# Moving the second batch's later pieces by eight visits, reordering ACT's ramp steps, and halving two products with their turns

## The chip, the cores and the metric

The kernel runs on one NeuronCore of a Trainium2 chip. Its engines work side by side, each through its own instruction list in order: PE (TensorE) multiplies matrices into the eight PSUM banks, ACT (ScalarE) and DVE (VectorE) read PSUM and SBUF, POOL (GpSimd) reads SBUF only, and SP (SyncE) issues the DMAs. An instruction that waits holds up everything behind it on its engine or queue. The metric is the device time of one execution in microseconds (us).

## The reference

For each of 4 batches of 12480 rows x of 128 numbers, two attentions and then a two-layer network:

```
h   = mab(I, x)          # 32 inducing rows attend to the batch
y   = mab(x, h)          # the batch attends to these 32 rows
# mab(q, kv): s = q kv^T / sqrt(128); a = softmax(s); a @ kv
g   = prelu(y @ w_in)    # 128 -> 2048, a slope alpha for each of the 2048
out = g @ w_out          # 2048 -> 128
```

Since y is a @ h with a of 32 columns, the kernel computes HW = h @ w_in once per batch, and then a @ HW in place of y @ w_in. The network's nonlinear part is relu(a @ HW) @ W1 with W1 = (1 - alpha) w_out; its linear part is a @ HA with HA = h @ (w_in alpha w_out).

## The kernel before

**Tiling.** A batch is cut into six rows of the schedule, called supers s = 0 to 5, of 16 tiles of 128 rows each, and a remainder of 192 rows. A super (b, s) of the second attention is four blocks of four tiles. The network of one block takes four visits; a visit makes 4 of the 16 chunks of the hidden layer. There are 390 visits in one chain: super (0, 0) has visits 0 to 15, (0, 1) has 16 to 31, (0, 2) has 32 to 47, (0, 3) begins at 48, and the second batch begins at visit 96.

**A visit** (`visit`, line 808): four matmuls `hh<-a,HW` that run side by side on 32 rows of the array each; four relus from PSUM into `gt` tiles, on ACT (line 821) or DVE (line 823); then `second` (line 834), the 16 matmuls of the visit before into the block's sums; and then the steps that hang on this visit. Every eighth visit, two blocks' linear parts (line 861) come between. A block's finished sums are copied into `ob` and stored by SP (lines 880 to 897).

**Steps.** `at(n, fn, ...)` hangs a step on visit n; steps of the same visit run in the order in which they were hung. A planner (`Plan`) goes through all visits with the steps' listed costs and chooses for each relu and copy whether ACT or DVE does it, and for each other step of these two engines whether it stays where it hangs or waits until after the second relu of the next visit (`plan.then`). It doesn't know POOL, the DMAs, or which step needs the result of which. What is hung on POOL and SP runs in the order of the list.

**A super of the second attention** takes these steps at the eight visits of `when`: `b_scores` (PE, line 644, and a copy out, lines 702 and 704), `b_max` (DVE, line 721), `b_less_pool` (POOL, line 726), `b_exp` (ACT, line 688), `b_sum` (POOL, lines 712 and 736), `b_rec` (DVE, line 749: one reciprocal for each softmax row), `b_mul` (POOL, line 757: exponentials times reciprocals, repeated four times into `rep`), and `b_turn` (SP, line 766: a transposing DMA of `rep` into the tile `a2`, "a" in the profile, which the visits' matmuls read). The one `rep` buffer of this kind serves all supers. For (0, 1) `when` is written out by hand, since there is no room for the usual lead of 23 visits. The first super (0, 0) is made in the ramp ahead of visit 0 and divides by its softmax sums only in the block's copy (line 880, with the reciprocals of `first_rec`, line 1173).

**The first attention of the next batch** is made between the visits in seven pieces p: p = 0 is super 0, p = 1 the remainder, p = 2 to 6 supers 1 to 5. Each piece has `a_load` (SP, line 315 or 320), a cast to bf16 (POOL, line 330; for p = 0 of the second batch four parts on ACT, line 347), `a_turn` (SP, line 356, a transposing DMA into `xT`), `a_scores_least` (PE line 379, DVE lines 393 and 402), `a_exp` (ACT, line 418), `a_e1` (SP, line 449, a transposing DMA), `a_fac` (ACT, line 436) and the join `a_h_add` (PE line 473, DVE lines 487 and 489). Behind the last join stand `a_max`, `a_factors`, `a_parts`, `a_den` (lines 508 to 573), `a_sum` (PE line 582, DVE line 587: the new h, `hT`), and `a_w_both` and `a_lin` (lines 598 to 621: HW and HA). The first `b_scores` of the second batch hangs on visit 73 and reads `hT`.

All loads, stores and transposing DMAs but the last store go through SP's one list, in the order in which the steps are hung.

Of the kernel before, what the change touches and what calls it, by code (L numbers as in the profile page):

```python
# [21 lines left out]
P = 128  # L22
R = 4
ST = 16
# [6 lines left out]
def kernel(  # L31
# [11 lines left out]
    bf16 = mybir.dt.bfloat16  # L43

    B, N, C = x.shape
    M = inducing.shape[0]
# [10 lines left out]
    if left:  # L57
        nt = -(-left // P)
        supers.append((len(supers) * ST * P, nt, left - (nt - 1) * P))
    NS = len(supers)  # L60
# [26 lines left out]
    H = ST // 2  # L87
# [14 lines left out]
    rep_pool = ctx.enter_context(tc.tile_pool(name="rep", bufs=1))  # L102
# [183 lines left out]
    def new_state(b):  # L286
        st = State()
        st.b = b
        st.pieces = whole_pieces if b else first_pieces
        st.np = len(st.pieces)  # L290
        st.xT = xt_pool.tile([C, NT, P], bf16, name="xT", tag="xT")
        st.xn, st.xs, st.s1, st.e1T, st.e1, st.s1p, st.hp = {}, {}, {}, {}, {}, {}, {}
        st.e2, st.m2, st.den2, st.rc, st.rep = {}, {}, {}, {}, {}

        st.mx = sm_pool.tile([P, NX], f32, name="mx", tag="mx")
        st.rm = sm_pool.tile([P, NX], f32, name="rm", tag="rm")
        st.fac = sm_pool.tile([P, NX], f32, name="fac", tag="fac")
        st.da = sm_pool.tile([P, NX], f32, name="da", tag="da")
        st.ex = sm_pool.tile([P, NX], f32, name="ex", tag="ex")
        st.den = sm_pool.tile([P, 1], f32, name="den", tag="den")  # L300
        st.hs = h_pool.tile([P, C], f32, name="hs", tag="hs")
        eng = nc.gpsimd if b else nc.vector
        eng.memset(st.mx[:], HIGH)
        eng.memset(st.da[:], 0.0)
        return st
# [320 lines left out]
    def a2_of(b, s):  # L626
        if (b, s) not in a2s:
            a2s[b, s] = a2_pool.tile([P, ST, P], bf16, name="a2", tag="a2")
        return a2s[b, s]
# [56 lines left out]
    def b_exp(e, n):  # L686
        def work():
            nc.scalar.activation(out=e[:, :n], in_=e[:, :n], func=EXP, scale=scale)  # L688

        plan.then(work)  # L690
# [60 lines left out]
        plan.then(work)  # L751
        st.rc[s] = rc

    def b_mul(st, s, n):
        rc = st.rc[s]
        rep = rep_pool.tile([P, ST, R, M], bf16, name="rep", tag="rep")
        nc.gpsimd.tensor_tensor(  # L757
            out=rep[:, :n],
            in0=st.e2[s][:, :n].unsqueeze(2).broadcast_to([P, n, R, M]),
            in1=rc[:, :n].unsqueeze(2).unsqueeze(3).broadcast_to([P, n, R, M]),  # L760
            op=MULT,
        )
        st.rep[s] = rep

    def b_turn(st, s, t0, n):
        nc.sync.dma_start_transpose(
            out=a2_of(st.b, s)[:, t0 : t0 + n, :],
            in_=st.rep[s][:, :n].rearrange("p t r m -> p (t r m)"),
        )

    def b_exp_once(e, n, w):
# [138 lines left out]
    st = new_state(0)  # L910
    xs_left = const.tile([P, supers[-1][1], C], f32, name="xs_left")
    for pc in first_pieces[:5]:
# [20 lines left out]
        out=mask[:], in_=ident32[:].rearrange("k (g m) -> k m g", g=R), axis=AX, op=ADD  # L933
# [3 lines left out]
        out=group[:], in_=ident32[:].rearrange("k (g m) -> k g m", g=R), axis=AX, op=ADD  # L937
# [5 lines left out]
        out=low[:], in0=mask[:], scalar1=-1.0, scalar2=HIGH, op0=ADD, op1=MULT  # L943
# [3 lines left out]
        out=nident[:], in0=ident32[:], scalar1=-1.0, scalar2=None, op0=MULT  # L947
# [255 lines left out]
    def at(n, fn, *args, cost=()):  # L1203


        todo.setdefault(max(n, 0), []).append((fn, args, cost))
# [1 line left out]
    at(2, rest_exp, H, H, cost=[("a", 560), ("!", 0)])  # L1208
    at(0, first_turn, cost=[("s", 350), ("f", 0)])
    at(2, first_turn_dma)  # L1210
    at(6, first_rec, cost=[("v", 160)])
    at(5, linear_product, cost=[("s", 900), ("v", 210), ("!", 0)])
    at(6, a_lin, st, cost=[("s", 260), ("v", 210)])
    blocks[0].later = True
# [4 lines left out]
    for b, s, nt in groups[1:]:  # L1219
        n = first[b, s]  # L1220
        when = [n - 23, n - 19, n - 16, n - 14, n - 13, n - 11, n - 9, n - 6]
        if (b, s) == (0, 1):
            when = [0, 2, 3, 4, 5, 8, 8, 8]
        if (b, s) == (0, 2):
            when[7] = n - 7
        at(when[0], on, b, b_scores, s, nt, cost=[("s", 25 * nt), ("f", 0)])
        at(when[1], on, b, b_max, s, nt, cost=[("v", 70 + 33 * nt)])
        at(when[2], on, b, b_less_pool, s, nt)
        at(
            when[3],  # L1230
            lambda b=b, s=s, nt=nt: b_exp(states[b].e2[s], nt),
            cost=[("a", 100 + 27 * nt)],
        )
        at(when[4], on, b, b_sum, s, nt)
        at(when[5], on, b, b_rec, s, nt, cost=[("v", 160)])
        at(when[6], on, b, b_mul, s, nt)
        at(when[7], on, b, b_turn, s, 0, nt)
    at(3, first_sum)
    for part in range(3):
        at(first[B, 0] - 50 + 8 * part, tails, part)  # L1240
# [3 lines left out]
    def small_at(n, fn, *args, cost):  # L1244


        (kind, ns), *rest = cost
        at(n, fn, *args, cost=[(kind, ns + (0 if n in shared else TURNED)), *rest])
        shared.add(n)

    for b in range(B - 1):
        n = first[b, 0] - 1
        if b:
            at(n - 4, lambda b=b: states.__setitem__(b + 1, new_state(b + 1)))
        for p, pc in enumerate(whole_pieces):
            m = n + (8 * (p - 1) if p > 1 else p)
            load, cast, turn = m - 3, m + 6, m + 8
            score = m + 15 if p > 1 else n + 16
            look = score + 1 + (p == 1)
            join = m + (24 if p == whole_pieces[-1].k else 23) if p > 1 else n + (31 if p else 23)  # L1260
            if not b:
                load, cast, turn = {
                    0: (-1, -1, 7), 1: (-1, 9, 10), 2: (4, 9, 11), 3: (12, 20, 21)
                }.get(p, (load, cast, turn))
                score, look = (score, look) if p > 1 else (score + 4, look + 4)
                join = n + 31 if p < 2 else n + 39 if p < 4 else join
            f = pc.full
            if load >= 0:
                at(load, on, b + 1, a_load, pc)
            if cast >= 0:  # L1270
                at(cast, on, b + 1, a_cast, pc)
            else:
                for q, v in enumerate((4, 5, 5, 6)):
                    at(v, on, b + 1, a_cast_act, pc, q * BT, BT, cost=[("a", 560)])
            at(turn, on, b + 1, a_turn, pc)
            small_at(
                score,
                on,
                b + 1,
                a_scores_least,  # L1280
                pc,
                cost=[("s", 215 if f else 85), ("v", 800 if f else 460)],
            )
            at(look, on, b + 1, a_exp, pc, cost=[("a", 717 if f else 430)])
            at(look + 2, on, b + 1, a_fac, pc, cost=[("a", 220)] if p else [])
            at(look + 1, on, b + 1, a_e1, pc)
            small_at(
                join, on, b + 1, a_h_add, pc, cost=[("s", 226 if f else 115), ("v", 260)]
            )
        m = n + 8 * (NS - 2) + 15  # L1290
        at(m + 2, on, b + 1, a_max, cost=[("a", 200)])
        at(m + 4, on, b + 1, a_factors, cost=[("s", 400), ("v", 70), ("a", 205)])
        at(m + 6, on, b + 1, a_parts, cost=[("a", 220), ("v", 260)])
        at(m + 8, on, b + 1, a_den, cost=[("s", 200), ("v", 370)])
        at(m + 12, on, b + 1, a_sum, cost=[("s", 200), ("v", 110)])
        small_at(m + 14, on, b + 1, a_w_both, cost=[("s", 220), ("a", 487)])
        small_at(m + 14, on, b + 1, a_lin, cost=[("s", 75), ("v", 190)])

# [3 lines left out]
    for n, (blk, i) in enumerate(visits):  # L1302
        before = visits[n - 1][0] if n else None
        nt = before.nt * before.per if n else 0
# [7 lines left out]
        cost = nt * Plan.FREE if both else 0  # L1312
# [55 lines left out]
```

## Time and profile before

| what | value |
|---|---|
| median of 3 runs | 596.29 us (595.6 to 596.78) |
| profiled execution | 597.49 us |
| its span | 595.6 us |
| PE busy | 585.8 us (98%) |
| DVE busy | 535.9 us (90%) |
| ACT busy | 537.4 us (90%) |
| POOL busy | 216.7 us (36%) |
| mean granted clock of TensorE | 0.997 |

The profile shows one execution. A row of the timeline has the start, the duration, the engine, the line, the operation with the tile written and those read, and the number of instructions merged; in brackets stands the engine's idle time ahead of it and what ended that. In the rows of SP the duration is that of the issue; when the transfer has landed is told by another view, the DMA issues, as the time from issue to landing. The granted clock is the share of full speed that TensorE was given.

### The profile page before, as it was taken

Reading aid. Unit: us, or ns where it says so; the run is one execution under the profiler, and the core shown is the slowest. Engines: PE = TensorE matmul, PEld = TensorE weight load, DVE = VectorE, ACT = ScalarE, POOL = GpSimd, SP = SyncE. Lnnn points to the kernel's source line nnn. Section 1 sums busy time; section 2 is a strip of 40 time slices with the busy share of each in tenths; the row PEclk is TensorE's granted clock in tenths of the full one; section 3 lists DMA queues with packets and bytes.
Section 4 is the critical chain, followed back from the end, with each engine's and each line's share of the span. In section 5 each row is a group of like instructions: output and inputs, shape, how many; then the busy total and the mean of one; then the engine's idle time right before and its main releaser. Section 6 shows DMA issues by size and latency. Waiting matters only on the chain.

```text
span 595.6 us, 23148 instructions
## 1 busy us (share of the span) xinstructions
PE 585.8 (98%) x9500; PEld 442.1 (74%) x9500; DVE 535.9 (90%) x978; ACT 537.4 (90%) x1085; POOL 216.7 (36%) x260
## 2 busy tenths in 40 slices
PE   9999979999999999999999999999999999999997
PEld 6677757777777777777777777777777777777776
DVE  5899979998999899989999989999999999999996
ACT  5789969999999999999989999999999999999986
POOL 3484615403416336223236165133133134144010
PEclk9999989999999999999999999999999999999999
DMA  8957999332167999641367989731331331433421
GB/s 337 274 171 148 245 228 195 74 100 72 56 185 173 223 199 215 134 82 39 89 150 174 202 213 227 167 82 55 90 73 55 91 63 65 118 73 68 91 69 47
DMA packets 122347, 80.56 MB, mean 135 GB/s; under 512 B 103760, under 2 KB 106112, under 8 KB 119168
## 3 DMA queue, kind: packets, MB, share of 16 engines
q1 hardware_dynamic: 122016, 78.99, 55.8%
q8 instruction: 74, 1.21, 0.9%
q14 instruction: 33, 0.27, 0.2%
q10 hardware_dynamic: 224, 0.09, 0.1%
HBM read 28.07 MB, written 25.56 MB: 90 GB/s over the span
## 4 chain that ended last, share of the span: by engine, by line
PE 94%; DMA 4%; DVE 1%; ACT 0%; issue 0%; DVEq 0%; POOL 0%; SPq 0%
PE bp L834 64%; PE hh L808 21%; DMA xs<-in_x_dram 3%; PE bp L861 2%; PE hh L644 2%; PE hh L473 1%; DMA a<-rep 1%; PE hh L379 1%; DVE gt L823 1%; PE bp L963 1%; PE hh L364 0%; PE hh L598 0%; PE hh L456 0%; DVEq L1363 0%; DVE xn L349 0%
## 5 line engine op out<-in xcount | busy, mean ns | idle before, releaser
L821 ACT ACTIVATE gt<-hh 128x512 bf16<-128x512 f32 x853 | 454.5, 604 | 39.2 <-PE hh L808 34.2
L823 DVE TENSOR_SCALAR gt<-hh 128x512 bf16<-128x512 f32 x707 | 454.1, 683 | 28.7 <-PE hh L808 17.6
L834 PE MATMUL bp<-W,gt 128*128 128x128 bf16 x6240 | 418.1, 220 | 0.2 <-DVE gt L823 0.2
L834 PEld LDWEIGHTS <-gt 128*128 128x128 bf16 x6240 | 350.4, 98 | 84.7 <-issue 77.2
L808 PE MATMUL hh<-a,HW 32*128 32x512 bf16 (+2 forms) x1664 | 156.8, 371 | 3.2 <-DMA a<-rep 3.1
L757 POOL TENSOR_TENSOR rep<-e,rc 128x2048 bf16<-128x2048 f32 (+1 forms) x24 | 84.5, 3521 | 24.4 <-DVE rc L749 23.4
L726 POOL TENSOR_TENSOR e<-e,smx 128x512 f32<-128x512 f32 (+1 forms) x24 | 24.6, 1026 | 154.6 <-ACT gt L821 88.6
L808 PEld LDWEIGHTS <-HW 32*128 32x128 bf16 x1664 | 40.5, 91 | 45.2 <-issue 6.3
L712 POOL TENSOR_TENSOR t<-e 128x256 f32<-128x256 f32 (+1 forms) x24 | 17.2, 718 | 144.4 <-ACT e L688 144.3
L887 ACT COPY ob<-bp 128x512 f32<-128x512 f32 (+1 forms) x62 | 36.3, 585 | 4.5 <-PE bp L834 1.6
L330 POOL CAST xn<-xs 128x2048 bf16<-128x2048 f32 x17 | 32.1, 1890 | 3.5 <-DMA xs<-in_x_dram 3.1
L712 POOL TENSOR_TENSOR t<-t 128x128 f32<-128x128 f32 (+3 forms) x100 | 30.4, 304 | 7.8
L889 DVE COPY ob<-bp 128x512 f32<-128x512 f32 x32 | 21.9, 684 | 6.1 <-PE bp L834 6.1
L393 DVE TENSOR_SCALAR_CACHE_REDUCE s<-hh 128x512 f32<-128x512 f32 (+2 forms) x29 | 17.9, 619 | 1.6 <-PE hh L379 1.6
L861 PEld LDWEIGHTS <-a 32*128 32x128 bf16 x392 | 15.0, 93 | 5.8 <-issue 0.2
L861 PE MATMUL bp<-HA,a 32*128 32x128 bf16 x392 | 19.1, 214 | 0.0
L418 ACT ACTIVATE e1T<-s,rm 128x512 bf16<-128x512 f32 (+1 forms) x25 | 17.9, 715 | 0.4 <-DVE rm L402 0.2
L721 DVE TENSOR_REDUCE smx<-e 128x16 f32<-128x512 f32 (+1 forms) x24 | 15.9, 661 | 0.0
L688 ACT ACTIVATE e<-e 128x512 f32<-128x512 f32 (+1 forms) x24 | 15.0, 624 | 0.8 <-POOL e L726 0.8
L963 PE MATMUL bp<-blank 128*128 128x256 bf16 x78 | 13.8, 311 | 1.2 <-DVE blank L909 1.2
L489 DVE SCALAR_TENSOR_TENSOR hs<-hs,fac,hh 128x128 f32<-128x128 f32 (+1 forms) x25 | 8.6, 344 | 6.2 <-PE hh L473 5.5
L702 ACT COPY e<-hh 128x512 f32<-128x512 f32 (+1 forms) x22 | 13.4, 607 | 0.0
(109 smaller groups left out, 204.1 us busy)
## 6 DMA issues: line engine op xcount, KB each, us to landing
out_dram<-ob SPq DMA_DIRECT2D x97, 256.0 KB, 2.6
xs<-in_x_dram SPq DMA_DIRECT2D x23, 1024.0 KB, 6.4
xs<-in_x_dram SPq DMA_DIRECT2D x2, 512.0 KB, 9.2
w_in_f<-in_moe_w_in_dram SPq DMA_DIRECT2D x1, 1024.0 KB, 4.8
a<-rep SPq DMA_TRANSPOSE x25, 4.9
xT<-xn SPq DMA_TRANSPOSE x18, 6.1
e<-e1T SPq DMA_TRANSPOSE x18, 3.1
xs_left<-in_x_dram SPq DMA_DIRECT2D x4, 64.0 KB, 5.1
```

The costliest lines, as they stand in the source:

```text
L330: nc.gpsimd.tensor_copy(out=st.xn[s][:], in_=xs[:])
L712: nc.gpsimd.tensor_tensor(out=t[:, :n], in0=src[:, :n, :w], in1=src[:, :n, w : 2 * w], op=ADD)
L726: nc.gpsimd.tensor_tensor(out=st.e2[s][:, :n], in0=st.e2[s][:, :n], in1=st.m2[s][:, :n].unsqueeze(2).broadcast_to([P, n, M]), op=SUB,)
L757: nc.gpsimd.tensor_tensor(out=rep[:, :n], in0=st.e2[s][:, :n].unsqueeze(2).broadcast_to([P, n, R, M]), in1=rc[:, :n].unsqueeze(2).unsqueez ...
L808: nc.tensor.matmul(hh[:, q * cols + w.start : q * cols + w.stop], HWs[b][rows, v * P : (v + 1) * P], a2[rows, t0 : t0 + nt, :].rearrange(" ...
L821: nc.scalar.activation(out=gt[:, :cols], in_=hh[:, :cols], func=RELU)
L823: nc.vector.tensor_relu(gt[:, :cols], hh[:, :cols])
L834: nc.tensor.matmul(blk.acc[:, t * C : (t + 1) * C], gt[:, (q * nt + t) * P : (q * nt + t + 1) * P], W1[:, k, :], start=(not blk.begun), st ...
L861: nc.tensor.matmul(blk.acc[w, t * C : (t + 1) * C], blk.a2[rows, blk.t0 + t, w], HAs[b][rows, :], start=(not blk.begun and t == 0), stop=F ...
L887: nc.scalar.copy(out=ob[:, :nt], in_=acc)
L889: nc.vector.tensor_copy(out=ob[:, :nt], in_=acc)
L963: nc.tensor.matmul(ps[:, : 2 * P], blank[:, :P], blank[:], start=True, stop=True)
```

## The change

- `b_mul` and `b_turn` work on `n` tiles from `t0`, and for (0, 1) and (0, 2) each is called for tiles 0 to 7 and for tiles 8 to 15. For (0, 1), where both hang on visit 8, the order is product, turn, product, turn; for (0, 2) the two products hang on visit 23 and the two turns on visit 25.
- For (0, 1) `b_exp` goes from visit 4 to 6 and `b_sum` from 5 to 7; the reciprocal, product and turn stay at 8. The four ACT casts of the second batch's piece 0 go from visits 4, 5, 5, 6 to 3, 4, 5, 5, its turn from 7 to 6, and `first_rec` from 6 to 7.
- In the second batch the pieces 3 to 6 come eight visits later in all their steps (piece 3's load, cast and turn go from 12, 20, 21 to 20, 29, 31; its join from 38 to 46), and so do the steps behind the last join, `a_sum` alone by six: from 66 to 72. `a_w_both` and `a_lin` go from 68 to 76.

```diff
-    def b_mul(st, s, n):
-        rc = st.rc[s]
-        rep = rep_pool.tile([P, ST, R, M], bf16, name="rep", tag="rep")
+    def b_mul(st, s, n, t0=0):
+        rc, ts = st.rc[s], slice(t0, t0 + n)
+        if not t0:
+            st.rep[s] = rep_pool.tile([P, ST, R, M], bf16, name="rep", tag="rep")
         nc.gpsimd.tensor_tensor(
-            out=rep[:, :n],
+            out=st.rep[s][:, ts],
...
     def b_turn(st, s, t0, n):
         nc.sync.dma_start_transpose(
             out=a2_of(st.b, s)[:, t0 : t0 + n, :],
-            in_=st.rep[s][:, :n].rearrange("p t r m -> p (t r m)"),
+            in_=st.rep[s][:, t0 : t0 + n].rearrange("p t r m -> p (t r m)"),
...
-    at(6, first_rec, cost=[("v", 160)])
+    at(7, first_rec, cost=[("v", 160)])
...
         if (b, s) == (0, 1):
-            when = [0, 2, 3, 4, 5, 8, 8, 8]
+            when = [0, 2, 3, 6, 7, 8, 8, 8]
...
-        at(when[6], on, b, b_mul, s, nt)
-        at(when[7], on, b, b_turn, s, 0, nt)
+        parts = [(0, H), (H, H)] if (b, s) in ((0, 1), (0, 2)) else [(0, nt)]
+        for t0, n in parts:
+            at(when[6], on, b, b_mul, s, n, t0)
+            if when[6] == when[7]:
+                at(when[7], on, b, b_turn, s, t0, n)
+        if when[6] != when[7]:
+            for t0, n in parts:
+                at(when[7], on, b, b_turn, s, t0, n)
...
-            m = n + (8 * (p - 1) if p > 1 else p)
+            m = n + (8 * (p - 1 + (not b and p > 2)) if p > 1 else p)
...
-                    0: (-1, -1, 7), 1: (-1, 9, 10), 2: (4, 9, 11), 3: (12, 20, 21)
+                    0: (-1, -1, 6), 1: (-1, 9, 10), 2: (4, 9, 11)
...
-                join = n + 31 if p < 2 else n + 39 if p < 4 else join
+                join = n + 31 if p < 2 else n + 39 if p < 3 else join
...
-                for q, v in enumerate((4, 5, 5, 6)):
+                for q, v in enumerate((3, 4, 5, 5)):
...
-        m = n + 8 * (NS - 2) + 15
+        m = n + 8 * (NS - 2 + (not b)) + 15
...
-        at(m + 12, on, b + 1, a_sum, cost=[("s", 200), ("v", 110)])
+        at(m + (12 if b else 10), on, b + 1, a_sum, cost=[("s", 200), ("v", 110)])
```

More of the change, by code (lines that the diff above doesn't have):

```diff
@@ L752, in b_rec @@
         st.rc[s] = rc
-    def b_mul(st, s, n):
-        rc = st.rc[s]
-        rep = rep_pool.tile([P, ST, R, M], bf16, name="rep", tag="rep")
+    def b_mul(st, s, n, t0=0):
+        rc, ts = st.rc[s], slice(t0, t0 + n)
+        if not t0:
+            st.rep[s] = rep_pool.tile([P, ST, R, M], bf16, name="rep", tag="rep")
         nc.gpsimd.tensor_tensor(
-            out=rep[:, :n],
-            in0=st.e2[s][:, :n].unsqueeze(2).broadcast_to([P, n, R, M]),
-            in1=rc[:, :n].unsqueeze(2).unsqueeze(3).broadcast_to([P, n, R, M]),
+            out=st.rep[s][:, ts],
+            in0=st.e2[s][:, ts].unsqueeze(2).broadcast_to([P, n, R, M]),
+            in1=rc[:, ts].unsqueeze(2).unsqueeze(3).broadcast_to([P, n, R, M]),
             op=MULT,
         )
-        st.rep[s] = rep
     def b_turn(st, s, t0, n):
```

## The prediction

> **What bounds the kernel now.** I read the page first, then the waits of PE, then the chain that ended last around the one large wait, then the queues behind it.
>
> ```profile
> span 595.6 us, 23148 instructions
> ...
> PE 585.8 (98%) x9500; PEld 442.1 (74%) x9500; DVE 535.9 (90%) x978; ACT 537.4 (90%) x1085; POOL 216.7 (36%) x260
> ...
> PE 94%; DMA 4%; DVE 1%; ACT 0%; issue 0%; DVEq 0%; POOL 0%; SPq 0%
> ```
>
> PE bounds it: 98% busy, and 94% of the chain. What can be won is PE's lost time. The waits of PE, and PE's timeline at the visits 31 to 35 (one row of `hh<-a,HW` opens each):
>
> ```profile
> PE hh L808 <- DMA a<-rep: 3.1, 1, 3.1
> ...
> 76.24 0.39 PE L808 MATMUL hh<-a,HW 32*128 32x512 bf16 x4
> 80.72 0.50 PE L808 MATMUL hh<-a,HW 32*128 32x512 bf16 x4 [3.09 <-DMA a<-rep]
> 82.98 0.61 PE L808 MATMUL hh<-a,HW 32*128 32x512 bf16 x4
> 84.88 0.39 PE L808 MATMUL hh<-a,HW 32*128 32x512 bf16 x4
> 86.20 0.40 PE L808 MATMUL hh<-a,HW 32*128 32x512 bf16 x4
> ```
>
> A plain visit takes 86.20 - 84.88 = 1.32 us. From visit 31 (76.24) to visit 34 (84.88) it took 8.64 where three plain visits take 3.97: 4.67 lost. 3.09 of it is idle ahead of visit 32, the first of super (0, 2), which waits for the turn of `rep` into `a`. The rest, 1.58, is slow work behind it, by the windows' granted clock (after the five engines' busy times):
>
> ```profile
> 77.60:80.70 3.10, 0.03 (x1) 0.00 (x0) 0.57 (x1) 0.70 (x2) 0.00 (x0) 1.00 1.43 144
> 80.70:83.00 2.30, 2.28 (x24) 1.75 (x24) 1.69 (x3) 1.30 (x3) 0.00 (x0) 0.54 0.88 285
> 83.00:85.00 2.00, 2.00 (x25) 1.43 (x24) 1.48 (x3) 1.32 (x3) 0.00 (x0) 0.68 1.09 278
> ```
>
> 0.54, then 0.68; from visit 34 on a visit takes 1.32 again. Why was the turn late? SP's list, POOL, and the end of ACT's exponential of piece 2:
>
> ```profile
> 59.53 0.89 SPq L315 DMA_DIRECT2D xs<-in_x_dram  x1
> ...
> 63.50 1.22 SPq L449 DMA_TRANSPOSE e<-e1T  x1
> 66.53 4.00 SPq L356 DMA_TRANSPOSE xT<-xn  x1
> 70.64 1.19 SPq L449 DMA_TRANSPOSE e<-e1T_left  x1
> 71.93 1.61 SPq L449 DMA_TRANSPOSE e<-e1T  x1
> 73.63 0.53 SPq L894 DMA_DIRECT2D out_dram<-ob  x1
> 74.25 3.11 SPq L766 DMA_TRANSPOSE a<-rep  x1
> ...
> 64.61 1.89 POOL L330 CAST xn<-xs 128x2048 bf16<-128x2048 f32 x1 [1.96 <-DMA xs<-in_x_dram]
> 66.47 3.61 POOL L757 TENSOR_TENSOR rep<-e,rc 128x2048 bf16<-128x2048 f32 x1
> ...
> 63.95 0.24 DVE L749 RECIPROCAL rc<-den 128x16 f32<-128x16 f32 x1
> ...
> 67.94 0.21 ACT L418 ACTIVATION_READ_ACCUMULATOR e1T<-s,rm 128x1 f32 x1
> ```
>
> The reciprocal was ready at 64.19, but POOL first cast piece 3 (waiting for its load till 64.61), so the product ended at 70.08. SP had piece 3's turn ahead, 4.00 us of issue from 66.53, so the two small turns behind it went out at 70.64 and 71.93, though ACT's last input to them was ready at 68.15. The product's turn went out at 74.25 and landed just ahead of 80.72, 6.4 later. The load at 59.53 is piece 4's.
>
> **The change part by part.** The sum is made against the profiled execution's 597.49 us (span 595.6, 1.89 around it); the median of the runs shown, 596.29, is 1.20 below, and the result is carried over by that.
>
> *Pieces 3 and 4 leave the way of (0, 2).* Piece 3's cast goes behind the product (visit 29 against 23), its turn (31) and piece 4's load (28) behind the turns (25). Piece 3's load stays ahead (20), about where 59.53 stands. The first half product can then start at 64.2. A half has 1024 elements; from the two forms of this product
>
> ```profile
> L757 POOL TENSOR_TENSOR rep<-e,rc 128x2048 bf16<-128x2048 f32 x23 | 83.0, 3610 | 22.0 <-DVE rc L749 21.0 <-PE hh L808 1.0
> L757 POOL TENSOR_TENSOR rep<-e,rc 128x768 bf16<-128x768 f32 x1 | 1.5, 1471 | 2.3 <-DVE rc L749 2.3
> ```
>
> it takes 1471 + 256 x (3610 - 1471)/1280 = 1899 ns (an estimate): halves end at 66.1 and 68.0, 0.19 more POOL work in all, on an engine 36% busy. SP then has e1 of piece 0 at 63.50, of piece 1 behind it, of piece 2 at 68.2 (its input), 1.3 of issue, the store 0.5, and the first half's turn at about 70.1. The nearest row of a half turn is the ramp's (line 1153), 1.25 of issue and 3.1 to landing; the whole one here took 6.4:
>
> ```profile
> a<-rep SPq DMA_TRANSPOSE x1, 3.1
> ...
> 37.50 1.25 SPq L1153 DMA_TRANSPOSE a<-rep  x1
> ```
>
> So the first half lands between 73.2 and 76.5; visit 32 needs it at 76.24 + 1.32 = 77.56, or at 77.1 with the ramp's gain (next). The second half follows 1.25 later and is needed only at visit 40, some 10 us after. The wait goes, and with it the low clock: -4.67. Bounds: 0, if DMA stays as full as before, and -4.67. I take the far end, since even the slow landing of 6.4 meets the need; the margin is 0.6 us there and 3.9 at best.
>
> *The ramp.* Visit 7, with its chain and what stood on ACT:
>
> ```profile
> 38.51 0.63 ACT L688 ACTIVATE e<-e 128x512 f32<-128x512 f32 x1 [0.84 <-POOL e L726]
> ...
> 39.56 0.61 ACT xn L347
> 40.17 0.99 ACT gt L821 x2
> ...
> 40.34 1.23 PE L808 MATMUL hh<-a,HW 32*128 32x512 bf16 x4
> ...
> 28.62 0.52 SPq L315 DMA_DIRECT2D xs<-in_x_dram  x1
> ...
> xs<-in_x_dram SPq DMA_DIRECT2D x1, 1024.0 KB, 5.7
> ```
>
> Four `hh` matmuls took 1.23 against 0.39: 0.84 lost, waiting for banks that ACT frees late, since it sat 0.84 for POOL ahead of the exponential and then had casts. With the casts ahead, from some 36 on (their load, issued at 28.62, landed 5.7 later at 34.3), the idle is filled, and at visit 6 the exponential finds POOL's input. Against it, the exponential now runs behind visit 6's relus, which ended at 41.16 here, so that it ends at 41 to 42 (an estimate) rather than at 39.1, and POOL's sum for (0, 1) may end up to one us later:
>
> ```profile
> 43.39 0.20 POOL L736 TENSOR_SCALAR den<-t 128x16 f32<-128x16 f32 x1
> 44.20 0.24 DVE L749 RECIPROCAL rc<-den 128x16 f32<-128x16 f32 x1
> ```
>
> The reciprocal at visit 8 had 0.6 of slack; with visit 8 earlier by 0.84 and the sum later, DVE may wait there by up to 1 us, with its relus behind it and PE behind these. Bounds -0.84 and +0.8; I take -0.5, nearer to the wait that the profile shows than to the one it doesn't. The turn of (0, 1) came in time for visit 16 as a whole (PE's waits have one for `a<-rep`, at visit 32); its first half now goes out behind half a product, so up to one us of delay in the sum is made good. `first_rec` a visit later has until the copy at visit 8, where it costs nothing.
>
> *The moved pieces' own cost.* Casts, DVE, ACT and PE work only move, into visits 36 to 76 whose PE was never idle. Each turn of pieces 4 to 6 hangs 3 visits ahead of a super's turn or behind it, as piece 5's (visit 39) did before (0, 3)'s (42). That one went out at 98.40, landed 4.6 later at 103.0, and was needed at visit 48:
>
> ```profile
> 98.40 2.33 SPq L766 DMA_TRANSPOSE a<-rep  x1
> ...
> a<-rep SPq DMA_TRANSPOSE x1, 4.6
> ...
> 105.61 0.40 PE L808 MATMUL hh<-a,HW 32*128 32x512 bf16 x4
> ```
>
> 2.6 of cover, which now has to hold with piece 4 in piece 5's place. I cost it at 0. Score and join of one piece leave visits 30 and 38 and reappear at 62 and 71: 0.
>
> *The end of the second batch's attention.* The last join (71), `a_sum` (72) and the first `b_scores` of the second batch (73) now follow visit by visit; before, 63, 66 and 73. If DVE lags, PE waits for `hs` at 72 and for `hT` at 73. In the trace of before:
>
> ```profile
> 129.40 0.35 DVE L489 SCALAR_TENSOR_TENSOR hs<-hs,fac,hh 128x128 f32<-128x128 f32 x1 [0.54 <-PE hh L473]
> ...
> 133.63 0.18 DVE L587 TENSOR_TENSOR hT<-hh,rec 128x32 bf16<-128x32 f32 x1
> ```
>
> DVE sat ready for the join's matmuls and added in 0.35; hT took 0.18; PE comes back for each a visit (1.32) later. So 0, or, where the planner puts DVE's step behind the second relu of the next visit, up to about 1 us each. Bounds 0 and +2.0; I take +0.2.
>
> *The planner* chooses anew for all visits. That can move small waits about; I take 0 and allow 1 us to either side.
>
> Sum: -4.67 - 0.5 + 0.2 = -4.97; 597.49 - 4.97 = 592.5 profiled, 591.3 as a median.
>
> **The rivals.** *The first half still comes late.* SP's way to it has two small turns and a store that wait for ACT; if these or DMA cost 2 us beyond the slow end, it lands at about 78.6 against a need at 77.1. PE then idles about 1.5; whether the clock falls decides between 1.5 and 1.5 + 1.58 lost. The result is 592.8 to 594.4. For it: DMA at 1.43 of its share in the wait; against: piece 4's load and piece 3's turn are out of it. On the clock, the trace has one case, 0.54 behind 3.09 idle.
>
> The Trainium skill, "TensorE: Matmul & The Clock Gate", Part 1 (The HAM clock gate), says that the clock drops after an idle window of about 3.4 us, free-running; its section "Why this matters for your kernels" warns of gaps of more than about 3 us. The 3.09 here already cost the clock, so the looser number is nearer; by that page a rest of 1.5 us would cost only itself, 592.8, and the sum of the likeliest case would be the same.
>
> *The stall moves to visit 48 (slower).* PE reaches visit 48 some 5 us earlier, and SP may not. Should (0, 3)'s turn come 2.6 us later against its visit than before, PE waits; beyond about 6 later the wait (3.4) and the low clock (1.58) take the whole gain. At 7 later: 4.4 + 1.58 - 4.97 = +1.0, a median of 597.3. For it: piece 4's turn, issued 3 visits ahead of it, is of the kind that took 4.00 above. Against: before, piece 5's turn stood at the same place, and by then one piece less has been moved.
>
> *The change doesn't do what it says*: if DMA is what sets the pace from 60 us on, the delayed loads and turns only take the wait to another super, of the same size: 596.3, no change.
>
> **How the numbers follow.** The likeliest case has 0.77, with a range of its own from 589.8 (ramp -0.84, end 0, planner -1) to 592.8 (ramp +0.2, end +1.0). The late half has 0.12, mostly faster; the stall at visit 48 has 0.08, slower; no change has 0.03. A measurement of this kernel tells about 0.2%, 1.2 us, from no change. Faster by over that: 0.77 + 0.11 = 0.88; within it 0.01 + 0.03 = 0.04; slower 0.08. The range goes from 589.8 to 594.2: it leaves out the slower case, no change, the top of the late half and some of the likeliest one's ends, 0.2 in all.
>
> **What would show it.** Right: no wait of PE for `a<-rep`; granted clock 1.00 from 75 to 90 us; visit 32 about 0.5 earlier than 77.56 and visit 34 about 5 earlier than 84.88; SP issuing two half turns near 70; no 1.23 at visit 7. Wrong: PE idle at visit 16, 32 or 48, a DVE wait for POOL's `den` near 44, or PE waiting at visits 72 and 73 for `hs` or `hT`.

## The result, and the profile after

The changed kernel takes 593.47 us (median of 5 runs, 593.18 to 593.93) against 596.29 before (595.6 to 596.78 in its 5 runs). The ratio is 0.9954, with a 95% interval of 0.9939 to 0.9968: 2.8 us or 0.46% faster. The profiled execution took 593.45 us with a span of 591.7, that is 4.04 us less than the profiled execution of before. Why the profiles differ by 4.0 and the medians by 2.8 is the main thing that the runs had to settle.

The page after the change, and its waits of PE (from the page: the span, the busy line, PE's busy tenths and the granted clock in 40 slices; then the first three rows of the list of PE's waits, with us in total, times and the longest; two more rows have 0.2 us each, for `gt` and `ind_b`):

```profile
span 591.7 us, 23147 instructions
...
PE 584.9 (99%) x9500; PEld 441.2 (75%) x9500; DVE 534.6 (90%) x977; ACT 537.8 (91%) x1086; POOL 216.9 (37%) x262
...
PE   8999999999999999999999999999999999999997
...
PEclk9999999999999999999999999999999999999999
```

```profile
PE bp L963 <- DVE blank L909: 1.2, 1, 1.2
PE hh L364 <- POOL w_in_f L1036: 0.7, 1, 0.7
PE hh L808 <- DVE ob L880: 0.2, 1, 0.2
```

The wait for `a<-rep` is gone from the list. A new small one stands there, for DVE's `ob`. PE's timeline at the visits 31 to 34, and SP's and POOL's around the turn of (0, 2), all after the change:

```profile
76.30 0.40 PE L808 MATMUL hh<-a,HW 32*128 32x512 bf16 x4
77.63 0.40 PE L808 MATMUL hh<-a,HW 32*128 32x512 bf16 x4
78.95 0.40 PE L808 MATMUL hh<-a,HW 32*128 32x512 bf16 x4
80.28 0.40 PE L808 MATMUL hh<-a,HW 32*128 32x512 bf16 x4
...
63.64 1.19 SPq L449 DMA_TRANSPOSE e<-e1T  x1
64.94 1.29 SPq L449 DMA_TRANSPOSE e<-e1T_left  x1
68.46 2.14 SPq L449 DMA_TRANSPOSE e<-e1T  x1
...
71.32 2.65 SPq L766 DMA_TRANSPOSE a<-rep  x2
74.02 0.57 SPq L315 DMA_DIRECT2D xs<-in_x_dram  x1
...
75.17 7.04 SPq L356 DMA_TRANSPOSE xT<-xn  x1
...
64.65 3.75 POOL L758 TENSOR_TENSOR rep<-e,rc 128x1024 bf16<-128x1024 f32 x2 [1.77 <-DVE rc L749]
...
a<-rep SPq DMA_TRANSPOSE x2, 3.2
```

The visits follow each other at 1.33 us. The three small turns no longer wait behind a turn of piece 3: the third goes out at 68.46, as soon as ACT has its input (68.44). The two halves go out at 71.32 (forecast 70.1), and the first lands 3.3 us later, at 74.6, which is 3.0 ahead of visit 32. A half product takes 1.88 us (3.75 / 2; estimated 1.90). The turn of piece 3, now behind, holds SP for 7.04 us.

To see where time went, I took from PE's timelines the start of every visit and counted, for each stretch of visits, the time over 1.326 us per visit. The work that lies between visits is in these sums too, so only differences count:

| visits | before | after | difference |
|---|---|---|---|
| 0 to 8 (mostly visit 7) | 1.85 | 1.04 | -0.81 |
| 8 to 16 | 0.83 | 1.87 | +1.04 |
| 16 to 31 | 2.40 | 2.24 | -0.16 |
| 31 to 34 | 4.66 | 0.00 | -4.66 |
| 34 to 48 | 2.17 | 1.95 | -0.22 |
| 48 to 78 | 3.87 | 4.56 | +0.69 |
| 78 to 100 | 0.85 | 1.15 | +0.30 |
| 100 to 389 | 26.64 | 26.42 | -0.22 |

Together -4.04. The loss in visits 8 to 16 is new; ACT's exponential of (0, 1) and the end of POOL's sum there, DVE's timeline, and PE's at visit 10:

```profile
41.28 0.62 ACT L688 ACTIVATE e<-e 128x512 f32<-128x512 f32 x1
44.33 0.20 POOL L736 TENSOR_SCALAR den<-t 128x16 f32<-128x16 f32 x1
...
42.18 1.28 DVE L823 TENSOR_SCALAR gt<-hh 128x512 bf16<-128x512 f32 x2
44.57 0.25 DVE L749 RECIPROCAL rc<-den 128x16 f32<-128x16 f32 x1 [1.10 <-POOL den L736]
44.74 1.22 DVE L880 TENSOR_TENSOR ob<-bp,rec 128x512 f32<-128x512 f32 x2
45.88 1.28 DVE L823 TENSOR_SCALAR gt<-hh 128x512 bf16<-128x512 f32 x2
...
44.95 0.86 PE L808 MATMUL hh<-a,HW 32*128 32x512 bf16 x3
46.02 0.37 PE L808 MATMUL hh<-a,HW 32*128 32x512 bf16 x1 [0.21 <-DVE ob L880]
```

DVE waits 1.10 us for POOL's sum ahead of the reciprocal of (0, 1); two block copies and the relus stand behind it, and PE's `hh` matmuls of visit 10 get their banks late (the four start over 1.07 us).

The rows of the table behind visit 78 need care. The +0.30 lies in visit 98 alone, whose four `hh` matmuls take 0.64 here and took 0.40 before. But in two of the experiments below, the halves alone and the ramp alone, visit 98 loses about 0.25 too, and the order of the operations on ACT and DVE from visit 78 on is the same in all nine traces of this document. Visit 98 before, after, and with the halves alone:

```profile
176.62 0.40 PE L808 MATMUL hh<-a,HW 32*128 32x512 bf16 x4
...
172.49 0.64 PE L808 MATMUL hh<-a,HW 32*128 32x512 bf16 x4
...
172.92 0.57 PE L808 MATMUL hh<-a,HW 32*128 32x512 bf16 x4
```

Behind visit 100 the nine traces lose between 26.1 and 26.9 us, so the -0.22 there can't be told from chance.

### The profile page after: what moved, and what is told of

Its sections match the earlier page's. It is cut to its first block, busy times and chain, and to the rows that moved or that the text cites. A ratio compares the mean times of both kernels' runs of the same rounds, so it can differ in the third digit from the quotient of the medians.

```text
span 591.7 us, 23147 instructions
## 1 busy us (share of the span) xinstructions
PE 584.9 (99%) x9500; PEld 441.2 (75%) x9500; DVE 534.6 (90%) x977; ACT 537.8 (91%) x1086; POOL 216.9 (37%) x262
## 4 chain that ended last, share of the span: by engine, by line
PE 91%; DVE 1%; DVEq 0%; issue 0%; ACT 0%
PE bp L834 64%; PE hh L808 21%; PE bp L861 2%; PE hh L644 1%; PE hh L473 1%; PE hh L379 1%; DVE gt L823 0%; DVE ob L880 0%; DVEq L1369 0%; PE hh L598 0%; PE hh L521 0%; DVE s L393 0%; PE hh L582 0%; PE hh L567 0%; PE hh L518 0%
## 5 line engine op out<-in xcount | busy, mean ns | idle before, releaser
L758 POOL TENSOR_TENSOR rep<-e,rc 128x2048 bf16<-128x2048 f32 (+2 forms) x26 | 84.8, 3263 | 24.6 <-DVE rc L749 24.2
L887 ACT COPY ob<-bp 128x512 f32<-128x512 f32 x64 | 37.5, 585 | 4.6 <-PE bp L834 1.4
L889 DVE COPY ob<-bp 128x512 f32<-128x512 f32 x30 | 20.6, 686 | 5.2 <-PE bp L834 5.2
```

The lines of the kernel that those rows point to most:

```text
L758: nc.gpsimd.tensor_tensor(out=st.rep[s][:, ts], in0=st.e2[s][:, ts].unsqueeze(2).broadcast_to([P, n, R, M]), in1=rc[:, ts].unsqueeze(2).un ...
L887: nc.scalar.copy(out=ob[:, :nt], in_=acc)
L889: nc.vector.tensor_copy(out=ob[:, :nt], in_=acc)
```

## The experiments

Each kernel was executed 5 to 12 times, beside the kernel before on the same chip; the ratios are to that.

**The kernel before, once more.** No edit.

> The kernel before, unchanged, in more executions. The profiled execution shown took 597.49 us, 1.2 over the median. Theory A: the wait of 3.1 us at visit 32 is the same in every execution, but whether the clock falls behind it is not; then other executions show a span of about 594.0 to 594.6, a mean granted clock of 0.999 rather than 0.997, and 4.66 - 1.2 = about 3.5 us or less lost at visits 31 to 33. Theory B: every execution loses 4.66 and the 1.2 us came from elsewhere; then the spans stay near 595.6 at 0.997, or the loss at visits 31 to 33 is 4.66 again where the time is 596.3.

Measured: 596.93 us as a median of 12, from 594.97 to 598.58, ratio 1.0005 (0.9992 to 1.0019); the kernel before beside the four runs, 596.37 as a median of 29, from 595.08 to 598.63. The profiled execution was the fastest, 594.97 us with a span of 593.2. Its wait of PE, its timeline at visits 31 to 34, and the windows' granted clock behind the wait (third from the end):

```profile
PE hh L808 <- DMA a<-rep: 2.2, 1, 2.2
...
75.91 0.40 PE L808 MATMUL hh<-a,HW 32*128 32x512 bf16 x4
79.47 0.40 PE L808 MATMUL hh<-a,HW 32*128 32x512 bf16 x4 [2.18 <-DMA a<-rep]
80.80 0.40 PE L808 MATMUL hh<-a,HW 32*128 32x512 bf16 x4
82.24 0.54 PE L808 MATMUL hh<-a,HW 32*128 32x512 bf16 x4
...
79.50:82.00 2.50, 2.50 (x38) 1.83 (x39) 2.03 (x4) 2.01 (x5) 0.00 (x0) 1.00 0.95 333
82.00:85.00 3.00, 3.00 (x44) 2.12 (x44) 3.00 (x6) 3.00 (x8) 0.40 (x1) 1.00 1.22 257
```

The same wait is 2.18 us here, and the clock doesn't fall. Visits 31 to 34 lose 2.35 in place of 4.66; the span is 2.4 shorter, and 2.31 of this lies in these three visits. So neither theory holds as written. Against A, the wait isn't the same in every execution, and the span is under the 594.0 that A gave; against B, the loss isn't 4.66 in every one. What holds of A is that an execution can lose 3.5 us or less there. The whole turn here went out at 73.29, 0.96 earlier than in the other trace, and landed after 6.1 us in place of 6.4; why the transfers differ was not tried. The spans of the 12 executions go from 593.2 to 596.8; the mean granted clock is 1.000 at 593.2 and 0.993 at both of the longest. It doesn't order them all: two spans of 595.1 come with 0.999 and 1.000. Only the fastest of the 12 was traced, so how much a middling one loses at visit 32 isn't shown.

**Only the later pieces.**

```diff
-        parts = [(0, H), (H, H)] if (b, s) in ((0, 1), (0, 2)) else [(0, nt)]
+        parts = [(0, nt)]
-    at(7, first_rec, cost=[("v", 160)])
+    at(6, first_rec, cost=[("v", 160)])
-            when = [0, 2, 3, 6, 7, 8, 8, 8]
+            when = [0, 2, 3, 4, 5, 8, 8, 8]
-                    0: (-1, -1, 6), 1: (-1, 9, 10), 2: (4, 9, 11)
+                    0: (-1, -1, 7), 1: (-1, 9, 10), 2: (4, 9, 11)
-                for q, v in enumerate((3, 4, 5, 5)):
+                for q, v in enumerate((4, 5, 5, 6)):
```

> Only the pieces 3 to 6 come eight visits later; whole products and turns, the ramp as before. The theory on record (piece 3's cast and turn stand ahead of (0, 2)'s product and turn in POOL's and SP's lists): the whole turn goes out near 70.5 and lands at 75 to 77, so no wait at visit 32 or under 0.5 us, and 592.8 to 593.5 as a median. Rival (the halving carries the gain): a whole product and turn still come late, 1 to 3 us of wait stay, and the time is 594.5 to 596.3.

Measured: 592.98 us (592.76 to 593.89), ratio 0.9946 (0.993 to 0.9963). No wait at visit 32; visits 31 to 34 lose 0.00. SP, PE and the landing of the whole turn:

```profile
64.60 1.19 SPq L449 DMA_TRANSPOSE e<-e1T_left  x1
67.99 1.19 SPq L449 DMA_TRANSPOSE e<-e1T  x1
...
70.29 2.80 SPq L766 DMA_TRANSPOSE a<-rep  x1
...
a<-rep SPq DMA_TRANSPOSE x1, 4.7
...
77.16 0.40 PE L808 MATMUL hh<-a,HW 32*128 32x512 bf16 x4
```

The whole turn lands at 75.0, 2.2 us ahead of visit 32. The later pieces alone are enough for the whole gain, with the landing and the time as expected. Piece 3's cast and turn and piece 4's load were moved together. The timelines say which of the two lists decided: in the profile before, the product had ended at 70.08 and SP reached its turn only at 74.25, so SP's order set the time there, and POOL's didn't. The later pieces have a price of their own: visits 16 to 31 -0.22, 34 to 48 -0.22, 48 to 78 +0.69, together +0.25. The changed kernel has 0.06 more, at visit 22, and so has the ramp's order alone.

**Only the halves.** The changed kernel with the pieces and the ramp as before (`when`, the steps of the ramp, the pieces' `m`, their table, join and end undone; two of the pairs are shown).

```diff
-            m = n + (8 * (p - 1 + (not b and p > 2)) if p > 1 else p)
+            m = n + (8 * (p - 1) if p > 1 else p)
...
-                    0: (-1, -1, 6), 1: (-1, 9, 10), 2: (4, 9, 11)
+                    0: (-1, -1, 7), 1: (-1, 9, 10), 2: (4, 9, 11), 3: (12, 20, 21)
```

> Only the halves for (0, 1) and (0, 2); pieces and ramp as before. The theory on record: SP still has piece 3's turn ahead, the first half goes out near 74.2 and lands 3.1 to 6.4 later, at 77.4 to 80.6, so 0 to 3 us of wait stay: 593.5 to 596.3. If the halving carries the gain: no wait at visit 32, 593 or less. A wait under 3 us also shows whether the clock falls behind a shorter wait.

Measured: 593.39 us as a median of 12, ratio 0.9955 (0.9938 to 0.9971); ten executions lie from 592.49 to 594.53, two at 596.61 and 596.85 with a clock of 0.997. In the profiled one visits 31 to 34 lose 0.13:

```profile
66.07 3.00 SPq L356 DMA_TRANSPOSE xT<-xn  x1
...
73.02 2.66 SPq L766 DMA_TRANSPOSE a<-rep  x2
...
DMA to landing us min/median/max: 3.3/3.4/3.6
...
78.25 0.39 PE L808 MATMUL hh<-a,HW 32*128 32x512 bf16 x4
```

SP still has piece 3's turn ahead, as the theory on record says, and the halves go out at 73.02. But the first, the slower of the two, lands 3.6 later, at 76.6, where whole turns needed 5.9 to 6.4 in the same place, and visit 32 begins at 78.25. A whole turn with 5.9 would have landed at 78.9, too late. So each part alone takes the wait away; my expectation had the half land at 77.4 or later. It is the shorter transfer that helps here, and not the shorter product: both products had ended at 69.0, 4.0 ahead of the turn. The cover of 1.6 is thinner than the 3.0 of the whole change. Whether the two long executions are late landings isn't shown; their traces weren't taken. The 0.13 isn't a rest of the wait: it lies in visit 33, and PE has no wait for `a<-rep`.

**Only the ramp.**

```diff
-    at(6, first_rec, cost=[("v", 160)])
+    at(7, first_rec, cost=[("v", 160)])
-            when = [0, 2, 3, 4, 5, 8, 8, 8]
+            when = [0, 2, 3, 6, 7, 8, 8, 8]
-                    0: (-1, -1, 7), 1: (-1, 9, 10), 2: (4, 9, 11), 3: (12, 20, 21)
+                    0: (-1, -1, 6), 1: (-1, 9, 10), 2: (4, 9, 11), 3: (12, 20, 21)
-                for q, v in enumerate((4, 5, 5, 6)):
+                for q, v in enumerate((3, 4, 5, 5)):
```

> Only the ramp's steps in the other order. Read from the two traces: 0.84 won at visit 7 and 1.05 lost at visit 10, where DVE waits 1.10 for POOL's sum, so +0.2: 596.3 to 596.8, with the wait at visit 32 still there. Rival (the ramp's order won as forecast and the loss at visit 10 comes from the halved product behind the reciprocal): no DVE wait for the sum, 595.4 to 595.8.

Measured: 597.6 us as a median of 12, ratio 1.002 (1.0007 to 1.0033): 1.2 slower, and 0.8 above the range expected. Visit 7 loses 0.03 in place of 0.84, visits 8 to 16 1.87 in place of 0.83, and the wait at visit 32 is there, 3.0 us. DVE waits for the sum with whole products as well, so the halved product isn't its cause:

```profile
PE hh L808 <- DMA a<-rep: 3.0, 1, 3.0
...
44.47 0.25 DVE L749 RECIPROCAL rc<-den 128x16 f32<-128x16 f32 x1 [1.10 <-POOL den L736]
```

The two visits explain +0.23 of the 1.2. Where the rest comes from isn't shown: the traced execution loses 4.61 at visits 31 to 34, as much as the profile before, and the kernel before has an execution that loses 2.35 there.

**The change without the ramp's order.** The last three pairs of the second diff, in the changed kernel.

> The change without the ramp's new order: later pieces and halves, the ACT casts, the exponential, the sum and the block reciprocals as before. If the ramp's order costs what the two traces say (0.8 won at visit 7, 1.05 lost at visit 10), this is about 0.2 faster than the whole change, at 593.0 to 593.3, with visit 7 losing 0.7 to 0.8 again and visit 10 nothing. If the halves lose what they are meant to win beside the later pieces (rival), it is over 593.5; if they add to the later pieces, under 592.8.

Measured: 592.88 us (592.66 to 593.71), ratio 0.9936 (0.9921 to 0.9951), just under the 593.0 to 593.3 expected. Visit 7 loses 0.86, visits 8 to 16 0.83. The halves add nothing that can be told beside the later pieces (592.98 without them), and the changed kernel with the ramp's order is 0.59 slower by the medians, with intervals of the ratios that overlap; by the visits, 0.21 of it lies in the ramp (visits 0 to 16) and 0.31 in visit 98, whose cause is open.

**The reciprocal of (0, 1) a visit later,** in the changed kernel.

```diff
-            when = [0, 2, 3, 6, 7, 8, 8, 8]
+            when = [0, 2, 3, 6, 7, 9, 9, 9]
```

> The whole change, but the reciprocal of (0, 1), its products and turns hang on visit 9 in place of 8. Theory: the loss at visit 10 is DVE waiting for POOL's sum ahead of this reciprocal (1.10 us), with the block copies and relus behind it; a visit later the sum is ready, so visits 8 to 16 lose about 0.8 as before the change, and the time is about 592.4. Rival: the loss comes from the order of copies and products on PE at visit 9; then it stays near 1.9, and the time stays at 593.4.

Measured: 592.38 us (592.3 to 592.51), ratio 0.9926 (0.9912 to 0.994). Visit 7 loses 0.04, visits 8 to 16 0.83. The copies now go ahead of the reciprocal, and its wait of 0.39 lies where the relus aren't late:

```profile
42.74 1.28 DVE L880 TENSOR_TENSOR ob<-bp,rec 128x512 f32<-128x512 f32 x2
43.94 0.68 DVE L823 TENSOR_SCALAR gt<-hh 128x512 bf16<-128x512 f32 x1
45.01 0.25 DVE L749 RECIPROCAL rc<-den 128x16 f32<-128x16 f32 x1 [0.39 <-POOL den L736]
```

**The exponential of (0, 1) a visit earlier,** in the changed kernel.

```diff
-            when = [0, 2, 3, 6, 7, 8, 8, 8]
+            when = [0, 2, 3, 5, 6, 8, 8, 8]
```

> The whole change, but the exponential of (0, 1) hangs on visit 5 and its sum on visit 6. The same theory from the other side: the exponential then ends near 39.0 (POOL gives its input at 38.4), POOL's sum follows the first super's without a gap and ends near 43.5 in place of 44.5, so DVE waits 0.2 or less: visits 0 to 8 lose 1.0 to 1.2, visits 8 to 16 0.8 to 1.1, and the time is 592.4 to 592.8. If ACT waits for POOL again ahead of the exponential, visit 7 loses up to 0.4.

Measured: 592.32 us (591.9 to 593.09), ratio 0.9926 (0.9911 to 0.9941). Visit 7 loses 0.12, visits 8 to 16 0.83. ACT runs the exponential between two casts, and DVE waits 0.42, more than the 0.2 expected but less than 1.10. The sum ends near 43.5 as forecast; the reciprocal comes earlier too, since DVE now has one relu ahead of it at that place where it had two:

```profile
37.80 0.63 ACT L347 CAST xn<-xs 128x512 bf16<-128x512 f32 x1
38.41 0.63 ACT L688 ACTIVATE e<-e 128x512 f32<-128x512 f32 x1
38.95 0.60 ACT L347 CAST xn<-xs 128x512 bf16<-128x512 f32 x1
...
43.53 0.25 DVE L749 RECIPROCAL rc<-den 128x16 f32<-128x16 f32 x1 [0.42 <-POOL den L736]
```

Both edits take the new loss away, from its two ends: the reciprocal came too early for a sum that came too late. These two kernels are the fastest of all, about 1 us under the changed one. In both the planner also divides the relus around the reciprocal anew, so its part in this isn't separated.

## Why the prediction was right or wrong

The direction, the cause and the place were right, and the time, 593.47, lies in the range (589.8 to 594.2) though not in the likeliest case's own (589.8 to 592.8). That it lies in the range is luck in part: the top, up to 594.2, was there for a first half that comes late, and the half came 3.0 us ahead of its need. The gain was 2.8 where 5.0 was forecast. By its steps:

- *Pieces 3 and 4 leave the way of (0, 2), -4.67.* The wait and the low clock went as forecast, 4.66 between the two profiles, and for the cause named: with the pieces alone moved it goes too. That the halves would do it alone wasn't seen: the first half landed after 3.3 us, and after 3.6 behind piece 3's turn, where the forecast left 3.1 to 6.4 open.
- *"The result is carried over by that"*, the 1.20 between the profiled execution and the median. This is the step that failed. It took the 4.67 of one execution for the loss in all of them, and put its 1.20 over the median elsewhere. The first run showed that the executions of before differ in this very wait: 2.18 us idle and full clock in one, 3.09 and a falling clock in the other, 2.31 us between them. The execution that the sum stood on was 1.20 above the median, so the loss in a middling one was nearer to 4.66 - 1.20 = 3.5, if that too lies in the wait, as it did in the one pair that was compared; no middling execution was traced, so the 3.5 is an estimate. The changed kernel hasn't that spread: its five executions lie within 0.75 us, and the profiled one is at their median.
- *The ramp, -0.5.* Wrong in sign, within its bounds (-0.84 to +0.8). Visit 7's 0.84 was won (the five traces with the old order lose 0.66 to 1.20 there, so this too differs between executions); the DVE wait for POOL's sum, named there with "up to 1 us", came with 1.10 and cost PE 1.04: +0.23. The forecast had named it as a sign of being wrong. I took the visible wait for the surer one, and gave the other too little weight; the row of the reciprocal had 0.6 of slack, and both shifts were in the text, visit 8 earlier by 0.84 and the sum later by up to one us (0.94 as measured, 44.33 against 43.39): 0.6 - 0.84 - 0.94 is a wait of about 1.2.
- *The moved pieces' own cost, 0.* It was +0.31 (-0.16, -0.22, +0.69 by the table), and it belongs to the later pieces: the +0.69 stands in all five traces that have them and in none of the four others. The moved score and join were the step costed at 0: visits 30 and 38 get shorter by 0.45 together and visits 62 and 71 longer by 0.69, while the other moved steps between 48 and 78 come out even. Why they cost more there was not tried.
- *The end of the second batch's attention, +0.2.* It cost nothing: PE has no wait for `hs` or `hT` of over 0.2 us.
- *The planner, 0 with 1 us to either side.* From visit 78 on it chose nothing else, by the order of the operations on ACT and DVE. The +0.30 in visit 98 and the -0.22 from 100 on aren't its work; the cause of the first is open, and the second is within what the traces differ by.

In the profiles the sum is -4.66 + 0.23 + 0.31 + 0.30 - 0.22 = -4.04 against the -4.97 forecast; the other 1.2 of the miss is the carrying over. The missing 0.9 of the sum is the ramp (0.73) and the price of the moved pieces (0.31), with 0.1 from visit 78 on, less the 0.2 set aside for the end of the attention. Of the rivals, the stall at visit 48 didn't come: after the change (0, 3)'s turn went out at 93.37, landed 4.9 later at 98.3, and was needed at 100.79, with 2.5 us of cover where 2.6 stood before.

```profile
93.37 3.40 SPq L766 DMA_TRANSPOSE a<-rep  x1
...
a<-rep SPq DMA_TRANSPOSE x1, 4.9
...
100.79 0.40 PE L808 MATMUL hh<-a,HW 32*128 32x512 bf16 x4
```

## What to carry to other kernels

The wait on a transfer was not a constant here (2.18, 3.0 and 3.09 us in three traces): before the removal of such a wait is priced, compare the profiled execution with the median, and where it lies above, take a second trace and see whether the wait was long in the first. When the reader of a result is moved earlier and its maker later, the slack between them closes from both sides; add both shifts and set them against the slack in the row. And where an engine in strict order waits for a small result, price everything that stands behind it: here 1.10 us ahead of a reciprocal of 0.25 cost PE nearly all of it.

## What the runs showed of the hardware

Ahead of visit 32 the TensorE clock stayed at 1.00 behind an idle time of 2.18 us and fell to 0.54 behind one of 3.09. The kernel with the ramp's order alone, 3.0 us idle, had a clock of 0.56 in the 2.3 us behind it and lost 4.61 in the same three visits, as much as the one with 3.09. So in these traces the limit lies between 2.2 and 3.0 us. The Trainium skill's "TensorE: Matmul & The Clock Gate" (Part 1) has an idle window of about 3.4 us for this. Both waits behind which the clock fell here are shorter than that, and the measurement decides.

The first half of (0, 2)'s transposing DMA (128x1024) landed 3.3 to 4.0 us after its issue in the five traces that have halves. The whole one (128x2048) took 4.7 with the pieces moved and 5.9 to 6.4 behind piece 3's turn. With the halves alone, this shorter way to the first half was what took the wait away.
